# Folding the states into two chunks of the weights at once

## The chip, the cores and the metric

The kernel runs on one core of a Trainium2 chip. The metric is the time of one execution on the device in microseconds (us), taken as the median of several runs. A hardware profile of one further execution gives the spans, the rows and the order of events that are read below. TensorE is called PE there, its weight loads PEld, VectorE DVE, ScalarE ACT, GpSimd POOL, and the engine that issues most of the transfers SP.

## What is computed

Three layers follow each other, all in fp32. The second is where the change lies:

```python
scores = scale * np.matmul(x, state.transpose(0, 1, 3, 2))
a = softmax(scores)
xread = np.matmul(a, state)
sread = np.matmul(softmax(scale * np.matmul(state, x.transpose(0, 1, 3, 2))), x)
attn_out = np.concatenate([xread, sread], axis=2)

x = attn_out.transpose(0, 2, 1, 3).reshape(B * S, H * D)
x = (x @ w_a) * (x @ w_b) @ w_out

out[mask] = gate_w[mask, None] * (np.maximum(x[mask] @ w1[e], 0.0) @ w2[e])
```

There are 8 batches of 8 heads with 512 rows and 32 states of 64 numbers each. Each batch has 544 rows of 512 numbers (512 of xread, 32 of sread) for the second layer, whose inner width is 1536. The third layer sends each row to one of 8 experts by an argmax over its logits.

## The kernel before

Since xread is a @ state, the product xread @ w_a equals a @ (state @ w_a). The kernel never forms xread: it multiplies the states into the weights first ("folds" them) and applies the softmax to the result. The folded weights differ from batch to batch.

The second layer runs in blocks of 512 rows. Blocks i = 0 to 7 are the xread rows of one batch each, block 8 holds the 256 sread rows of all batches. The inner width is cut into 12 chunks, fc = 0 to 11, of 128 columns each of w_a and of w_b. A step is one chunk of one block, numbered 12 i + fc. `run` issues in each step what the string `STEP` lists:

```python
STEP = "mm1 fold a gc gm fh sg lt p mm2 lm b"
```

- `mm1` multiplies the block's softmax, split into a high and a low part AH and AL, by the folded weights of this chunk: 12 matmuls of 512 columns into the PSUM tiles pa and pb. Block 8 has plain weights, 256 rows and no fold.
- `fold` prepares the chunk two steps ahead. It multiplies the states by a chunk of the weights: 8 matmuls in fp32, for 4 pairs of heads j and 2 heads g, each on 64 rows and 32 columns of the array, with 256 columns moving (128 of w_a and 128 of w_b). They end in two PSUM tiles pm, one for each g.
- `gc` (copy_a) copies pa to SBUF on ScalarE; `gm` (times_b) multiplies it by pb on VectorE; `sg` splits the product into gh (ScalarE) and gl (VectorE).
- `fh` (folded) splits pm into high and low part: for each g a copy by ScalarE and a subtraction by VectorE, into a tile mm.
- `mm2` multiplies the product of the step before by w_out: 12 matmuls of 512 columns into po.
- `lt` and `lm` turn the finished rows of the block before for the logits (steps 1 to 4 of a block); `a`, `p` and `b` are places at which the attention of the next batch is issued (`PLAN`, `BATCH`): scores in step 0, directly behind the fold; the transposition of the second softmax (turn_s) in steps 3 and 7, its product with x (sread) in steps 4 and 8. `gate` runs after step 6 and `place`, which counts the ranks of the rows with matmuls of its own, after step 7.

Each engine works through its own queue in order. From step 14 to step 106 the order of the queues is that of the program; before and behind, a scheduler sets it. The tiles of pool `ps` (pa, pb, pm, and those of scores, turns and ranks, tag "ps") share four PSUM buffers of 2 KB in turn, so a new tile waits until the tile four places before it has been read. The pool `b2` gives mm two buffers.

The weights arrive as 64-bit numbers and are converted in the first block (`conv_pre`, `conv`) into one tile `ab0` to `ab11` of 4 KB for each chunk. In block 8 these are split on ScalarE and GpSimd (`split_w`), and the places of those no longer needed take the weights of the first expert, 16 tiles e0 to e15 of 4 KB, in the order of `SPACE` and not before the step that `READY` sets (`split_e0`). The third layer follows with queues of its own (`moe2`).

Of the kernel before, what the change touches and what calls it, by code (L numbers as in the profile page):

```python
# [7 lines left out]
F32 = mybir.dt.float32  # L8
F32R = mybir.dt.float32r
BF16 = mybir.dt.bfloat16  # L10
I32 = mybir.dt.int32
# [4 lines left out]
ALU = mybir.AluOpType  # L16
# [3 lines left out]
P = 128  # L20
# [8 lines left out]
CX = 320  # L29
# [20 lines left out]
)  # L50

SPACE = "ab0 ab1 wo0 ab2 ab3 wo1 ab4 wo2 ab5 ab6 wo3 ab7 ab8 ab9 ab10 ab11".split()
READY = 0, 0, 4, 6, 8, 9, 11, 12, 13, 14, 15, 16

BATCH = ("- - -", "- 0a 4p", "-2b -7a 0p")
# [2 lines left out]
def chunk(raw, c):  # L58
    g = raw[c // 2]
    return g[0][0][:, (c % 2) * 512 : (c % 2) * 512 + 512] if len(g) == 1 else g[c % 2][0]  # L60


class Front:


    def __init__(self, tc, ctx, xT, xN, sT, wab, wo, wgN, w1c, w2c, xs):
        self.__dict__.update(tc=tc, nc=tc.nc, xT=xT, xN=xN, sT=sT, wab=wab, wo=wo, wgN=wgN, w1c=w1c, w2c=w2c, xs=xs)
        nc = tc.nc
        self.V, self.A, self.G, self.PE = nc.vector, nc.scalar, nc.gpsimd, nc.tensor
        pool = lambda name, bufs, **kw: ctx.enter_context(tc.tile_pool(name=name, bufs=bufs, **kw))  # L70
        self.ctx = ctx
        self.cp = pool("c", 1)
        self.dp = pool("dram", 1, space=bass.MemoryType.DRAM)
        self.wp = pool("w", 1)
        self.p1 = pool("b1", 1)
        self.p2 = pool("b2", 2)
        self.at = pool("at", 2)
        self.ps = pool("psb", 4, space=PSUM)
        self.pso = pool("pso", 1, space=PSUM)
        self.sctx = ExitStack()  # L80
        self.sp = self.sctx.enter_context(tc.tile_pool(name="stg", bufs=2))
        self.us, self.xt, self.st, self.AB, self.WO, self.cvq, self.cvp = {}, {}, {}, {}, {}, [], []
        self.cvo = [0, 1] + [q for f in range(1, NF) for q in (3 * f, 3 * f + 1, 3 * f - 1)] + [3 * NF - 1]
        self.ahl, self.pm, self.MM = {}, {}, {}
        self.pab, self.g2, self.po, self.rows, self.lg, self.gt, self.ix, self.tp = {}, {}, {}, {}, {}, {}, {}, {}
        self.blocks = [(i * 512, 512) for i in range(8)] + [(4096, 256)]
        self.consts()
# [147 lines left out]
    def conv_pre(self):  # L235

        if not self.cvq:
            return
        q, raw = self.cvq.pop(0)
        fc, m = divmod(q, 3)  # L240
        r32 = raw.bitcast(I32).rearrange("p (n t) -> p n t", t=2)
        hi, lo = r32[:, :, 1], r32[:, :, 0]
        if m == 0:
            self.AB[fc] = self.wp.tile([P, 2, 512], I32, name=f"ab{fc}")
        w = self.AB[fc][:, m] if m < 2 else self.sp.tile([P, 512], I32, name="wt")
        self.A.activation(w.bitcast(F32), hi.bitcast(F32), AF.Copy, scale=2.0**-112)
        self.cvp.append((q, w, hi, lo))
# [15 lines left out]

    def fold(self, i, fc):

        pm = self.pm[i, fc] = [self.ps.tile([P, 256], F32, name=f"pm{g}", tag="ps") for g in range(2)]
        w, s = self.AB[fc].bitcast(F32), self.st[i]
        for j in range(4):
            for g in range(2):
                z = slice(64 * g, 64 * g + 64)  # L270
                self.PE.matmul(pm[g][32 * j : 32 * j + 32], s[z, j], w[z, :, j * P : j * P + P], start=True, stop=True)  # L271

    def folded(self, i, fc):
        m = self.MM[i, fc] = self.p2.tile([P, 2, 2, 256], F32R, name="mm")
        for g, t in enumerate(self.pm.pop((i, fc))):
            self.A.copy(m[:, 0, g], t)  # L276
            self.V.tensor_tensor(m[:, 1, g], t, m[:, 0, g], op=ALU.subtract)  # L277

    def load_xs(self):
        self.xsr = [self.at.tile([P, 2, 256], F32, name=f"xsr{a}", tag="eT") for a in range(2)]  # L280
# [82 lines left out]
    def turn_t(self, i, t, tag="ps"):  # L363

        tp = (self.ps if tag == "ps" else self.pso).tile([P, 512], F32, name="tp", tag=tag)
        for k in range(4):
            self.PE.transpose(tp[:, k * P : k * P + P], self.rows[i][:, t, k * P : k * P + P], self.ident)
        if t == 0:
            nt = self.blocks[i][1] // P
            self.x2 = self.lp.tile([P, 4, 512], F32, name="x2T") if nt == 4 else self.p2.tile([P, 2, 512], F32, name="x2T8", tag="mm")  # L370
        x = self.x2[:, t]
        if t % 2 == 0:
            self.A.copy(x, tp)
        else:
            self.V.tensor_copy(x, tp)
        self.tp[i] = tp
# [55 lines left out]

    def unit0_rows(self):
        p2 = self.p2
        r = p2.tile([P, 8, P], F32, name="rows0", tag="mm")
        self.load_rows(0, CW, r)
        xT = p2.tile([P, 1024], F32, name="xT0", tag="mm")
        th, tl = [p2.tile([P, 4, 8, 32], F32R, name=f"x0{n}", tag=n) for n in ("AH", "AL")]
        self.x0 = [[t[:, k] for k in range(4)] for t in (th, tl)]

        def turn0():
            self.turn_first(r, xT)
            self.turn_rows(1024, xT, *self.x0)

        self.turn0 = turn0
        self.mt = self.cp.tile([P, 3, 3, 2], F32, name="mt")
        r0 = self.first(0, E * REG - CW)
        self.m0 = self.cp.tile([P, 2, 2], F32, name="m0")
        self.nc.sync.dma_start(self.m0, self.xs[bass.ds(r0, CW), DM:RW].rearrange("(t p) c -> p t c", p=P))
# [96 lines left out]
    def split_e0(self):  # L546
        c = len(self.WH)
        if c >= 16:
            return
        t = self.wp.tile([P, 2, 512], F32R, name=f"e{c}", tag=SPACE[c])  # L550
        h, l = t[:, 0], t[:, 1]
        r = chunk(self.raw, c)
        self.A.copy(h, r)
        self.V.tensor_tensor(l, r, h, op=ALU.subtract)
        self.WH.append(h)
        self.WL.append(l)
# [140 lines left out]
    def run(self, order):  # L697
# [4 lines left out]
        def go(when):  # L702
            for f, a in sched.pop((st, when), []):
                f(*a)
# [22 lines left out]
        def logit():  # L727
# [4 lines left out]
            mm1=lambda: self.mm1(i, fc),  # L732
            mm2=second,
            fold=lambda: fold(self.fold),
            fh=lambda: fold(self.folded),
            gc=lambda: self.copy_a(i, fc),
            gm=lambda: self.times_b(i, fc),
# [6 lines left out]
            p=lambda: go("p"),  # L744
# [45 lines left out]
        i = nb - 1  # L790
# [10 lines left out]
        for t in range(2):  # L801
# [17 lines left out]
        self.unit0_mm2(0)  # L819
        self.unit0_mm2(1)  # L820
        x3 = self.lp.tile([P, 3, 2, CX], F32R, name="x3", tag="rows")
        x2 = [x3[:, k] for k in range(3)] + [self.p2.tile([P, 2, CX], F32R, name="x2", tag="mm")]
        xTh, xTl = [[x[:, q].rearrange("p (g t) -> p g t", t=32) for x in x2] for q in range(2)]
        self.turn_rows(4 * CX, wk[:, 2], xTh, xTl)
        self.mk = [self.PE.value_load(self.tab[0:1, 5 * NT + q : 5 * NT + q + 1], min_val=(0, 15)[q == 3], max_val=(2**NU - 1, NU)[q == 3]) for q in range(4)]
# [6 lines left out]
            xT=wk[:, 2],  # L832
            x2=x2,
# [437 lines left out]
```

## Time and profile before

| | |
|---|---|
| median of 3 runs | 1187.0 us (1183.28 to 1187.92) |
| profiled execution | 1186.3 us, span from first to last instruction 1184.5 us |
| TensorE busy | 1125.2 us, 95% of the span |
| VectorE busy | 751.1 us, 63% |
| ScalarE busy | 547.8 us, 46% |
| GpSimd busy | 242.6 us, 20% |
[...]

The times of runs include what lies around the span, 1.8 us in the profiled execution. The shares are means over stages that differ: conversion of the weights up to about 119 us, the blocks up to about 695 us, then block 8, the turn to the experts and the third layer.

### The profile page before, as it was taken

The numbers are of one execution on the slowest core, as the hardware profiler recorded it, in microseconds if no ns is written. First come the engines' busy times: TensorE is split into PE (matmuls) and PEld (weight loads), VectorE is DVE, ScalarE is ACT, GpSimd is POOL, SyncE is SP. The second block draws the span as 40 slices with busy tenths as digits, with TensorE's granted clock in tenths as the row PEclk, the third lists the DMA queues.
The fourth block names the chain that finished last, engine by engine and source line by source line (L and its number), as shares of the span: only waits on it lengthen the run. The fifth ranks groups of instructions, "written<-read, shape, count | busy, mean of one in ns | idle before, by whom it ended". The sixth has DMA issues, their size and how long they took to land. (4 is left out here: it accounts for less than half of the span.)

```text
span 1184.5 us, 21232 instructions
## 1 busy us (share of the span) xinstructions
PE 1125.2 (95%) x7867; PEld 899.3 (76%) x7867; DVE 751.1 (63%) x1585; ACT 547.8 (46%) x1171; POOL 242.6 (20%) x229
## 2 busy tenths in 40 slices
PE   3898999999999999999999998999999999999995
PEld 1565677777777777777777787889989898998995
DVE  6998554563664554555644436656887897777774
ACT  4554433432433333323333244425766767667663
POOL 1111001001000010010010143512434443434432
PEclk9998999999999999999999999999999999999998
DMA  7673822012011120120010041222765753154620
GB/s 288 191 247 120 183 53 75 1 37 76 1 50 63 38 63 15 38 75 1 2 55 1 19 143 37 59 62 62 205 192 165 220 160 101 43 170 95 186 59 26
DMA packets 68106, 108.79 MB, mean 92 GB/s; under 512 B 17266, under 2 KB 44146, under 8 KB 67970
## 3 DMA queue, kind: packets, MB, share of 16 engines
q1 hardware_dynamic: 61714, 89.11, 26.3%
q0 software_dynamic: 6256, 17.94, 4.0%
q8 instruction: 77, 1.26, 0.4%
q14 instruction: 59, 0.48, 0.1%
HBM read 83.30 MB, written 25.68 MB: 92 GB/s over the span
## 5 line engine op out<-in xcount | busy, mean ns | idle before, releaser
L322 DVE TENSOR_TENSOR g<-g,pb 128x512 f32<-128x512 f32 (+1 forms) x108 | 70.9, 656 | 222.1 <-PE pb L313 222.1
L337 PE MATMUL po<-wo,gh 128*128 128x512 f32 x408 | 170.9, 419 | 7.3 <-ACT gh L137 7.3
L318 ACT COPY g<-pa 128x512 f32<-128x512 f32 (+1 forms) x108 | 60.6, 561 | 227.8 <-PE pa L313 227.5
L338 PE MATMUL po<-wo,gh 128*128 128x512 f32 x408 | 161.4, 396 | 0.0
L339 PE MATMUL po<-wo,gl 128*128 128x512 f32 x408 | 159.8, 395 | 0.0
L524 POOL DMA_INDIRECT xs<-rows,ix x34 | 35.8, 1053 | 549.8 <-DVE AL L138 396.3
L978 PE MATMUL ph<-x,e 128*128 128x256 f32 (+1 forms) x480 | 138.6, 289 | 6.7 <-DVE e L1133 3.8
L980 PE MATMUL ph<-x,e 128*128 128x256 f32 (+1 forms) x480 | 138.7, 289 | 0.0
L979 PE MATMUL ph<-x,e 128*128 128x256 f32 (+1 forms) x480 | 138.5, 288 | 0.0
L276 ACT CAST mm<-pm 128x256 fp32r<-128x256 f32 x192 | 62.5, 375 | 122.3 <-PE pm L271 122.3
L337 PEld LDWEIGHTS po<-wo,gh 128*128 128x128 f32 x408 | 77.1, 189 | 44.9 <-issue 21.1
L978 PEld LDWEIGHTS ph<-x,e 128*128 128x128 f32 x480 | 91.7, 191 | 8.4 <-issue 7.9
L996 PE MATMUL pq<-e,h 128*128 128x512 f32 x240 | 93.4, 389 | 0.0
L995 PE MATMUL pq<-e,h 128*128 128x512 f32 x240 | 93.4, 389 | 0.0
L997 PE MATMUL pq<-e,h 128*128 128x512 f32 x240 | 93.4, 389 | 0.0
L979 PEld LDWEIGHTS ph<-x,e 128*128 128x128 f32 x480 | 91.6, 191 | 0.5
L980 PEld LDWEIGHTS ph<-x,e 128*128 128x128 f32 x480 | 91.8, 191 | 0.0
L339 PEld LDWEIGHTS po<-wo,gl 128*128 128x128 f32 x408 | 76.9, 189 | 18.7 <-DVE gl L138 0.8
L1166 DVE SCALAR_TENSOR_TENSOR h<-ph,h 128x256 fp32r<-128x256 f32 x120 | 50.5, 423 | 59.1 <-ACT h L1098 58.8
L338 PEld LDWEIGHTS po<-wo,gh 128*128 128x128 f32 x408 | 77.5, 190 | 13.1
L277 DVE TENSOR_TENSOR mm<-pm,mm 128x256 fp32r<-128x256 f32 x192 | 72.7, 418 | 22.2 <-ACT mm L276 22.2
L271 PE MATMUL pm<-ab,sT 64*32 64x256 f32 x1536 | 65.4, 398 | 18.8 <-DVE ab L258 17.0
(250 smaller groups left out, 2536.9 us busy)
## 6 DMA issues: line engine op xcount, KB each, us to landing
raw<-in_wab_dram SPq DMA_DIRECT2D x24, 512.0 KB, 4.4
wk<-xs SPq DMA_DIRECT2D x76, 160.0 KB, 3.7
xT<-in_xT_dram SPq DMA_DIRECT2D x16, 512.0 KB, 4.9
xn<-in_xN_dram SPq DMA_DIRECT2D x16, 512.0 KB, 4.6
er_x<-in_w1c_dram SPq DMA_DIRECT2D x16, 512.0 KB, 4.3
er_xn<-in_w1c_dram SPq DMA_DIRECT2D x16, 512.0 KB, 6.1
er_se<-in_w2c_dram SPq DMA_DIRECT2D x16, 512.0 KB, 4.5
er_y<-in_w2c_dram SPq DMA_DIRECT2D x16, 512.0 KB, 4.6
```

Of the source, the lines that this page charges most:

```text
L271: self.PE.matmul(pm[g][32 * j : 32 * j + 32], s[z, j], w[z, :, j * P : j * P + P], start=True, stop=True)
L277: self.V.tensor_tensor(m[:, 1, g], t, m[:, 0, g], op=ALU.subtract)
L322: self.V.tensor_tensor(g[:, :n], g[:, :n], pb[:, :n], op=ALU.mult)
L337: PE.matmul(o, gh[:, s], O[:, 0], start=fc == 0, stop=False)
L338: PE.matmul(o, gh[:, s], O[:, 1], start=False, stop=False)
L339: PE.matmul(o, gl[:, s], O[:, 0], start=False, stop=fc == NF - 1)
L978: e.matmul(o, WH[fc][:, c], xh, start=k == 0, stop=False)
L979: e.matmul(o, WL[fc][:, c], xh, start=False, stop=False)
L980: i = e.matmul(o, WH[fc][:, c], xl, start=False, stop=k == 3)
L995: e.matmul(o, hh[fc][:, z], WH[8 + fc], start=fc == 0, stop=False)
L996: e.matmul(o, hl[fc][:, z], WH[8 + fc], start=False, stop=False)
L997: i = e.matmul(o, hh[fc][:, z], WL[8 + fc], start=False, stop=fc == 7)
```

## The change

From block 1 on, `fold` works on two chunks at once in every even step, and does nothing in the odd ones. Its 8 matmuls have 512 moving columns, 256 of each chunk, and the two pm tiles fill a whole PSUM buffer. `folded` then splits both chunks in the same step, so the tag mm has three buffers. So that one access can reach two chunks, the converted weights lie in six tiles of two chunks (8 KB). The expert's tiles take them by halves, in another order (`SPACE`); e0 to e15 are due in the same steps. Block 0 folds chunk by chunk as before.

```diff
-SPACE = "ab0 ab1 wo0 ab2 ab3 wo1 ab4 wo2 ab5 ab6 wo3 ab7 ab8 ab9 ab10 ab11".split()
+SPACE = "ab0 ab0 ab1 ab1 wo0 wo1 ab2 ab2 wo2 wo3 ab3 ab3 ab4 ab4 ab5 ab5".split()
...
         if m == 0:
-            self.AB[fc] = self.wp.tile([P, 2, 512], I32, name=f"ab{fc}")
+            if fc % 2 == 0:
+                self.AB2[fc // 2] = self.wp.tile([P, 2, 2, 512], I32, name=f"ab{fc // 2}")
+            self.AB[fc] = self.AB2[fc // 2][:, fc % 2]
...
     def fold(self, i, fc):
 
-        pm = self.pm[i, fc] = [self.ps.tile([P, 256], F32, name=f"pm{g}", tag="ps") for g in range(2)]
-        w, s = self.AB[fc].bitcast(F32), self.st[i]
+        nf = 2 if i else 1
+        if fc % nf:
+            return
+        pm = [self.ps.tile([P, nf, 256], F32, name=f"pm{g}", tag="ps") for g in range(2)]
+        w, s = self.AB2[fc // 2].bitcast(F32)[:, fc % 2 : fc % 2 + nf], self.st[i]
         for j in range(4):
             for g in range(2):
                 z = slice(64 * g, 64 * g + 64)
-                self.PE.matmul(pm[g][32 * j : 32 * j + 32], s[z, j], w[z, :, j * P : j * P + P], start=True, stop=True)
+                o = pm[g][32 * j : 32 * j + 32].rearrange("p f (m c) -> p f m c", m=2)
+                self.PE.matmul(o, s[z, j], w[z, :, :, j * P : j * P + P], start=True, stop=True)
+        for f in range(nf):
+            self.pm[i, fc + f] = [t[:, f] for t in pm]
 
     def folded(self, i, fc):
-        m = self.MM[i, fc] = self.p2.tile([P, 2, 2, 256], F32R, name="mm")
-        for g, t in enumerate(self.pm.pop((i, fc))):
-            self.A.copy(m[:, 0, g], t)
-            self.V.tensor_tensor(m[:, 1, g], t, m[:, 0, g], op=ALU.subtract)
+        if i and fc % 2:
+            return
+        for f in range(fc, fc + (2 if i else 1)):
+            m = self.MM[i, f] = self.p2.tile([P, 2, 2, 256], F32R, name="mm", bufs=3)
+            for g, t in enumerate(self.pm.pop((i, f))):
+                self.A.copy(m[:, 0, g], t)
+                self.V.tensor_tensor(m[:, 1, g], t, m[:, 0, g], op=ALU.subtract)
...
-        t = self.wp.tile([P, 2, 512], F32R, name=f"e{c}", tag=SPACE[c])
+        k = SPACE[c]
+        if k[0] == "w":
+            t = self.wp.tile([P, 2, 512], F32R, name=f"e{c}", tag=k)
+        else:
+            if k not in self.e2:
+                self.e2[k] = self.wp.tile([P, 2, 2, 512], F32R, name=f"e{c}", tag=k)
+            t = self.e2[k][:, int(SPACE[c - 1] == k) if c else 0]
```

The lines of the changed program are numbered some 6 to 17 higher. The queue of TensorE in step 6 of block 5, from the last matmul of mm1 over the fold to the first of mm2, stands before as

```order
L313 MATMUL pb<-AL,mm 128x512
L271 MATMUL pm_4831<-ab_774,sT 32x256
L271 MATMUL pm_4832<-ab_774,sT 32x256
...
L337 MATMUL po_4523<-wo_665,gh 128x512
L338 MATMUL po_4523<-wo_665,gh 128x512
```

and now as

```order
L324 MATMUL pb<-AL,mm 128x512
L277 MATMUL pm_4545<-ab_770,sT 32x512
L277 MATMUL pm_4546<-ab_770,sT 32x512
...
L348 MATMUL po_4257<-wo_662,gh 128x512
L349 MATMUL po_4257<-wo_662,gh 128x512
```

The eight matmuls stay where they were and have 512 columns. In step 7 of the same block, the same queue, from mm1 over the turn of the softmax (pt) to mm2, stands before as

```order
L313 MATMUL pb<-AL,mm 128x512
L271 MATMUL pm_4904<-ab_855,sT 32x256
L271 MATMUL pm_4905<-ab_855,sT 32x256
...
L197 MATMUL pt<-ident,se 128x128 x4
L337 MATMUL po_4523<-wo_769,gh 128x512
```

and now as

```order
L323 MATMUL pb<-AH,mm 128x512
L324 MATMUL pb<-AL,mm 128x512
L197 MATMUL pt<-ident,se 128x128 x4
L348 MATMUL po_4257<-wo_765,gh 128x512
L349 MATMUL po_4257<-wo_765,gh 128x512
```

The fold of step 7 is gone. On VectorE the same two steps, from times_b (g) of step 6 over the softmax's normalization (sm, se) and the gate (down to rows) to the low part of g in step 7, stand before as

```order
L322 TENSOR_TENSOR g<-g,pb 128x512
L277 TENSOR_TENSOR mm<-pm_4831,mm 128x256
L277 TENSOR_TENSOR mm<-pm_4832,mm 128x256
L138 TENSOR_TENSOR gl<-g,gh 128x512
L182 TENSOR_SCALAR sm<-sm 128x1
...
L500 RECIPROCAL rows<-gm 128x4
L322 TENSOR_TENSOR g<-g,pb 128x512
L277 TENSOR_TENSOR mm<-pm_4904,mm 128x256
L277 TENSOR_TENSOR mm<-pm_4905,mm 128x256
L138 TENSOR_TENSOR gl<-g,gh 128x512
```

and now as

```order
L333 TENSOR_TENSOR g<-g,pb 128x512
L288 TENSOR_TENSOR mm<-pm_4545,mm 128x256
L288 TENSOR_TENSOR mm<-pm_4546,mm 128x256
L288 TENSOR_TENSOR mm<-pm_4545,mm 128x256
L288 TENSOR_TENSOR mm<-pm_4546,mm 128x256
L138 TENSOR_TENSOR gl<-g,gh 128x512
L182 TENSOR_SCALAR sm<-sm 128x1
...
L511 RECIPROCAL rows<-gm 128x4
L333 TENSOR_TENSOR g<-g,pb 128x512
L138 TENSOR_TENSOR gl<-g,gh 128x512
```

The two subtractions of step 7 stand in step 6 now, ahead of the low part of g and of all that follows it; ScalarE's copies moved in the same way. The queues of GpSimd and SP hold the same instructions in the same order.

## Rows read from the trace of the kernel before

**Rows 1.** Busy time by stage: us, then each engine's busy us (xinstructions), granted clock, DMA.

```profile
119.00:695.00 576.00, 576.00 (x4298) 420.78 (x4298) 301.24 (x728) 202.27 (x450) 35.71 (x44) 1.00 0.17 50
...
690.00:1184.50 494.50, 469.38 (x3009) 428.01 (x3007) 346.03 (x648) 287.83 (x610) 191.69 (x153) 0.98 0.40 114
```

**Rows 2.** Timeline, TensorE, a fold ahead of mm2: start us, us, instruction.

```profile
501.42 0.39 PE L312 MATMUL pb<-AH,mm 128*128 128x512 f32 x1
501.65 0.39 PE L313 MATMUL pb<-AL,mm 128*128 128x512 f32 x1
501.97 0.66 PE L271 MATMUL pm<-ab,sT 64*32 64x256 f32 x16
502.56 0.50 PE L337 MATMUL po<-wo,gh 128*128 128x512 f32 x1
502.90 0.39 PE L338 MATMUL po<-wo,gh 128*128 128x512 f32 x1
```

**Rows 3.** Timeline, TensorE, a fold ahead of turn_t.

```profile
554.85 0.39 PE L313 MATMUL pb<-AL,mm 128*128 128x512 f32 x1
555.17 0.66 PE L271 MATMUL pm<-ab,sT 64*32 64x256 f32 x16
555.77 0.66 PE L367 MATMUL tp<-ident,rows 128*128 128x128 f32 x4
556.18 0.48 PE L337 MATMUL po<-wo,gh 128*128 128x512 f32 x1
556.49 0.39 PE L338 MATMUL po<-wo,gh 128*128 128x512 f32 x1
```

**Rows 4.** Timeline, TensorE, turn_t in block 8, without a fold.

```profile
705.43 0.60 PE L367 MATMUL tp<-ident,rows 128*128 128x128 f32 x4
705.78 0.48 PE L337 MATMUL po<-wo,gh 128*128 128x512 f32 x1
706.10 0.39 PE L338 MATMUL po<-wo,gh 128*128 128x512 f32 x1
```

**Rows 5.** Timeline, TensorE, a fold ahead of the scores, then mm2.

```profile
540.83 0.66 PE L271 MATMUL pm<-ab,sT 64*32 64x256 f32 x16
541.29 1.55 PE L147 MATMUL ss<-xT,sT 64*32 64x512 f32 x16
542.77 0.51 PE L337 MATMUL po<-wo,gh 128*128 128x512 f32 x1
```

**Rows 6.** Instructions of the fold's and the scores' line: ns minimum/median/maximum, first and last start.

```profile
L271 PE MATMUL pm<-ab,sT x1536: 372/400/632, 14.7 to 682.7; 64*32 64x256 f32 x192
...
L147 PE MATMUL ss<-xT,sT x128: 589/613/1057, 6.0 to 542.2; 64*32 64x512 f32 x128
```

**Rows 7.** Timeline, TensorE, what is in flight at 541.6 to 541.7, and at 541.73 to 542.19.

```profile
541.29 0.59 PE L147 MATMUL ss<-xT,sT 64*32 64x512 f32 x1
...
541.29 1.12 PE L147 MATMUL ss<-xT,sT 64*32 64x512 f32 x9
```

**Rows 8.** Timeline, VectorE, times_b in the step with the scores; idle time in brackets.

```profile
541.01 0.69 DVE L322 TENSOR_TENSOR g<-g,pb 128x512 f32<-128x512 f32 x1 [3.82 <-PE pb L313]
```

**Rows 9.** Timeline, VectorE, steps 6 and 7 of block 5.

```profile
503.12 0.76 DVE L277 TENSOR_TENSOR mm<-pm,mm 128x256 fp32r<-128x256 f32 x2 [0.29 <-ACT mm L276]
...
508.45 0.56 DVE L497 TENSOR_TENSOR pre<-pre,oh 128x8 bf16<-128x8 bf16 x3
...
509.44 0.67 DVE L322 TENSOR_TENSOR g<-g,pb 128x512 f32<-128x512 f32 x1
```

**Rows 10.** Groups by line, 119 to 690 us: xcount | busy us, mean ns | idle us before.

```profile
L322 DVE TENSOR_TENSOR g<-g,pb 128x512 f32<-128x512 f32 x85 | 58.4, 687 | 208.0 <-PE pb L313 208.0
```

**Rows 11.** Timeline, TensorE, the rank matmuls after step 7 of block 5.

```profile
512.10 0.19 PE L509 MATMUL pk<-oh,tri 128*128 128x32 bf16 x1
```

**Rows 12.** Timeline, GpSimd (chunk 3 split) and ScalarE (e0 to e3), block 8.

```profile
707.64 2.54 POOL L138 TENSOR_TENSOR ws<-ab,ws 128x512 fp32r<-128x512 f32 x2 [1.85 <-ACT ws L137]
...
712.19 2.18 ACT L553 CAST e<-er_x 128x512 fp32r<-128x512 f32 x4
```

More of the change, by code (lines that the diff above doesn't have):

```diff
@@ L83, in __init__ @@
         self.cvo = [0, 1] + [q for f in range(1, NF) for q in (3 * f, 3 * f + 1, 3 * f - 1)] + [3 * NF - 1]
-        self.ahl, self.pm, self.MM = {}, {}, {}
+        self.ahl, self.pm, self.MM, self.AB2, self.e2 = {}, {}, {}, {}, {}
         self.pab, self.g2, self.po, self.rows, self.lg, self.gt, self.ix, self.tp = {}, {}, {}, {}, {}, {}, {}, {}
@@ L369, in turn_t @@
             nt = self.blocks[i][1] // P
-            self.x2 = self.lp.tile([P, 4, 512], F32, name="x2T") if nt == 4 else self.p2.tile([P, 2, 512], F32, name="x2T8", tag="mm")
+            self.x2 = self.lp.tile([P, 4, 512], F32, name="x2T") if nt == 4 else self.p2.tile([P, 2, 512], F32, name="x2T8", tag="mm", bufs=3)
         x = self.x2[:, t]
@@ L434, in unit0_rows @@
         p2 = self.p2
-        r = p2.tile([P, 8, P], F32, name="rows0", tag="mm")
+        r = p2.tile([P, 8, P], F32, name="rows0", tag="mm", bufs=3)
         self.load_rows(0, CW, r)
-        xT = p2.tile([P, 1024], F32, name="xT0", tag="mm")
+        xT = p2.tile([P, 1024], F32, name="xT0", tag="mm", bufs=3)
         th, tl = [p2.tile([P, 4, 8, 32], F32R, name=f"x0{n}", tag=n) for n in ("AH", "AL")]
@@ L821, in run @@
         x3 = self.lp.tile([P, 3, 2, CX], F32R, name="x3", tag="rows")
-        x2 = [x3[:, k] for k in range(3)] + [self.p2.tile([P, 2, CX], F32R, name="x2", tag="mm")]
+        x2 = [x3[:, k] for k in range(3)] + [self.p2.tile([P, 2, CX], F32R, name="x2", tag="mm", bufs=3)]
         xTh, xTl = [[x[:, q].rearrange("p (g t) -> p g t", t=32) for x in x2] for q in range(2)]
```

## The prediction

> **What bounds the kernel now.** I read four views, from coarse to fine. The stages come first: from 119 to 695 us TensorE is busy in all of 576 us at a granted clock of 1.00, while VectorE has work for 301 us and ScalarE for 202 [rows 1]. So nearly half of the kernel is a stretch in which TensorE never waits, and a microsecond taken off its queue there is a microsecond of the end, as long as nobody else starts to be waited for. Behind it, from 690 us on, TensorE is busy for 469 of 494.5 us [rows 1]; that part begins when the stretch ends.
>
> Then the timeline of TensorE around a fold, for what one fold costs the queue. The dense matmuls of 512 columns follow each other every 0.23 us. A fold that stands between mm1 and mm2 breaks that pace: from the start of the last mm1 matmul (501.65) to that of the second mm2 matmul (502.90) pass 1.25 us [rows 2], where two steps of the pace would take 0.46. **One fold costs 0.79 us.** Its 16 instructions (8 matmuls, two each for fp32) are shorter than that looks: where a group of the same 64x32 tiling follows, it starts 541.29 - 540.83 = 0.46 us after the fold does [rows 5], though one instruction alone lasts 0.40 [rows 6]. Eight run at once, in two rounds, and the rest of the 0.79 is leaving and entering the tiling.
>
> Where four transpositions follow the fold (turn_t, turn_s), the same distance is 556.49 - 554.85 = 1.64 us [rows 3]. In the last block, which has no fold, the first of them starts 706.10 - 705.43 = 0.67 us ahead of the second mm2 matmul [rows 4]; with one step of 0.23 from a 512-column matmul that is 0.90. A fold there costs 0.74 us.
>
> **The change, part by part.**
> *The odd steps lose their fold.* There are 42 such steps (11, 13, ... 93). In 22 the fold stands directly ahead of mm2, in 20 ahead of transpositions (14 of turn_t, 6 of turn_s). Taken off the queue: 22 x 0.79 + 20 x 0.74 = 32.2 us. It all lies on TensorE's queue in the stretch where TensorE is the bound.
>
> *The even steps get matmuls of 512 columns in place of 256.* No row of before shows a fold of 512 columns, but the scores have this very form: 64 rows, 32 columns of weights, 512 moving. One of their instructions has a median of 613 ns against 400 for the fold, and at the minimum 589 against 372 [rows 6]: 0.21 more either way. Two rounds make 0.43 us more for a fold. That it could be less no row suggests, since twice the columns have to pass. The other end is the whole group of scores: 542.77 - 541.29 = 1.48 us [rows 5], against 502.56 - 501.97 = 0.59 for a fold [rows 2], 0.89 more. I take 0.43: in the scores only one instruction is in flight at 541.6 us, and from 541.73 on the others come together [rows 7], and times_b, which frees the buffer of the second scores tile, runs from 541.01 for 0.69 us, to 541.70 [rows 8]. So the group's extra time is a wait for that buffer. The fold's two buffers were freed a step earlier. 36 even steps x 0.43 = 15.5 us.
>
> *In the other 6 even steps the scores follow the fold.* The larger fold takes 0.46 + 0.43 there and the scores start at 541.72 instead of 541.29, when times_b has just ended. Without the wait they need what a 512-column fold needs, 0.59 + 0.43 = 1.02, so mm2 starts at 542.74, against 542.77 now. I put these six at 0, with 0.43 each as the other end.
>
> **The sum:** 32.2 - 15.5 = 16.7 us less. The profiled execution took 1186.3 us (span 1184.5), which gives 1169.6; its time is 0.7 us below the median of 1187.0, so I say 1170.
>
> *The evacuation comes in fours.* Its instructions are the same in number and shape; what moves is when. In an even step the DVE queue holds four subtractions between times_b and the low part of g, and an odd step none. A pair of them takes 0.76 us [rows 9], so the last ends 0.43 (the larger fold) + 0.76 = 1.19 us later than now. Who waits for that? In most steps VectorE has stood idle before times_b, 208.0 us over 85 of them or 2.4 each [rows 10], and the buffers are wanted a step later: cost nothing, and the cover is that idle time. The tight place is step 6 of a block, where the softmax's normalization and the gate stand behind the subtractions. There times_b of step 7 starts at 509.44 [rows 9], without idle time before it, and the gate's last sum for the ranks (L497) is done at 508.45 + 0.56 = 509.01. TensorE wants it at 512.10 [rows 11]: 3.1 us of slack. After the change that sum is done 1.19 later, at 510.20, and TensorE arrives 0.74 - 0.43 = 0.31 earlier, at 511.79. 1.6 us are left, so I cost it at nothing.
>
> *The third buffer of mm* lets the copies of a pair be written while the second chunk of the last pair is still to be read; no new wait comes from it.
>
> *The weight tiles of two chunks* are reused in pairs by the first expert's tiles in the last block. The first pair whose turn is tight is e2 and e3 in the place of chunks 2 and 3: GpSimd splits chunk 3 from 707.64 for 2.54 us, to 710.18, and the copies of e0 to e3 start at 712.19 [rows 12]. 2 us of slack: cost nothing. SP and POOL issue what they issued.
>
> **The rivals.**
> *Part is given back at the gate.* If VectorE or ScalarE is later than I reckon in step 6, TensorE waits at the rank matmuls. For it: VectorE's queue has no idle time there. Against: the 1.6 us. If it costs the full shift of 1.19 + 0.31 = 1.5 us in each of 7 blocks, 10.5 us go back: 1180.
>
> *The larger folds cost what the scores cost.* If 0.89 is a property of 512 columns and not a wait, the even steps pay 42 x 0.89 = 37.4 us, more than the 32.2 saved: 1191.5, 0.4% above now. Against it stands that a single instruction is alone in flight until times_b ends [rows 7, 8].
>
> *The gain is lost behind the stretch.* If something after 690 us waited for a transfer and not for TensorE, the end would stay: 1186. Against: TensorE is busy for 95% of that part.
>
> *VectorE becomes the bound, the slower side.* Four subtractions in a row hold up times_b and the low part of g; if this makes mm1 or mm2 of the next step wait in every even step, 42 x 1.19 = 50 us are added: 1186.3 - 16.7 + 50 = 1220. It decides once the 2.4 us of idle time before times_b are used up; VectorE's 52% in the stretch speaks against that. [...]
>
> **How the numbers follow.** The forecast has 0.76, the gate 0.11, the costly folds 0.05, the loss behind the stretch 0.04, VectorE as the bound 0.04. The forecast's own range comes from 0.05 us of doubt on 84 prices, 4 us: 1165 to 1174. With the gate's case the range is 1165 to 1180, and 0.13 is left outside. A measurement can tell a change of about 0.5%, some 6 us, from none: forecast and gate are faster by more, 0.87; the costly folds and the loss behind it are within, 0.09; VectorE as the bound is slower, 0.04.
>
> **What would show it.** In the profile after: half as many fold instructions in the stretch, of 512 columns and about 0.61 us; a distance of about 1.68 us from the last mm1 matmul to the second mm2 matmul in an even step, 0.46 in an odd one; TensorE busy throughout a stretch some 16 us shorter; the scores' group shorter than 1.48 us; the rank matmuls about 1.6 us behind the gate's last sum. I am wrong if folds of 512 columns last as a group 1.4 us or more, if idle time of TensorE appears ahead of the rank matmuls, mm1 or mm2 with VectorE as its releaser, or if the part behind the stretch grows by what the stretch lost.

## The result and the profile after

The changed kernel takes 1174.57 us (median of 6 runs, 1172.52 to 1179.71) against 1187.29 in the runs of the kernel before beside it (1183.28 to 1189.23). The ratio is 0.991, interval 0.989 to 0.9929: 12.7 us less, where the prediction had 1170 and 16.7. The profiled execution took 1174.63 us, its span 1172.8.

The timeline of TensorE in steps 5 to 7 of block 5 answers to [rows 2]. First comes step 5, without a fold (last matmul of mm1, first two of mm2), then step 6 with the pair, then the turn of the softmax and the first rank matmul of step 7:

```profile
486.00 0.39 PE L324 MATMUL pb<-AL,mm 128*128 128x512 f32 x1
486.23 0.40 PE L348 MATMUL po<-wo,gh 128*128 128x512 f32 x1
486.46 0.40 PE L349 MATMUL po<-wo,gh 128*128 128x512 f32 x1
...
491.53 0.39 PE L324 MATMUL pb<-AL,mm 128*128 128x512 f32 x1
491.85 1.09 PE L277 MATMUL pm<-ab,sT 64*32 64x512 f32 x16
492.87 0.50 PE L348 MATMUL po<-wo,gh 128*128 128x512 f32 x1
493.21 0.39 PE L349 MATMUL po<-wo,gh 128*128 128x512 f32 x1
...
498.48 0.60 PE L197 MATMUL pt<-ident,se 128*128 128x128 f32 x4
...
501.69 0.19 PE L520 MATMUL pk<-oh,tri 128*128 128x32 bf16 x1
```

From mm1's last matmul to mm2's second pass 0.46 us in the odd step and 493.21 - 491.53 = 1.68 in the even one, the two numbers that the prediction named. Where the scores follow the fold (the same view, to be held against [rows 5]), the lone scores instruction is gone, the group lasts 531.70 - 530.64 = 1.06 us, and from the fold to mm2 pass 1.94 us as before:

```profile
529.76 1.09 PE L277 MATMUL pm<-ab,sT 64*32 64x512 f32 x16
530.64 1.12 PE L147 MATMUL ss<-xT,sT 64*32 64x512 f32 x16
531.70 0.51 PE L348 MATMUL po<-wo,gh 128*128 128x512 f32 x1
```

The line of the fold (beside [rows 6]) has 864 instructions instead of 1536, with a median of 589 ns; the forms are a sample:

```profile
L277 PE MATMUL pm<-ab,sT x864: 373/589/632, 14.8 to 662.2; 64*32 64x512 f32 x134, 64*32 64x256 f32 x39
```

VectorE has 164.3 us of idle time before 85 times_b, 1.9 each, instead of the 2.4 of [rows 10] (groups by line, 119 to 675 us):

```profile
L333 DVE TENSOR_TENSOR g<-g,pb 128x512 f32<-128x512 f32 x85 | 58.4, 687 | 164.3 <-PE pb L324 161.2 <-ACT g L329 1.7 <-issue 0.3
```

The turn_t of block 8 without a fold, at 705.43 in [rows 4], comes at 690.70, 14.7 us earlier:

```profile
690.70 0.60 PE L378 MATMUL tp<-ident,rows 128*128 128x128 f32 x4
```

So up to there all went as predicted. Put matmul beside matmul in the two traces, and the lead is 16.2 us at 860 us of the kernel before, 14.2 at 900, and 11.3 from 960 to the last unit. That it first grows from 14.7 to 16.2 is not the change's doing: the kernel before has one stretch more at the lower level of TensorE's clock (0.50 of full speed for 3.4 us, from 723.73 on), behind 3.73 us of which TensorE was busy for 1.47. The column behind POOL is the granted clock:

```profile
723.80:727.00 3.20, 3.04 (x37) 2.69 (x38) 1.06 (x4) 1.03 (x2) 2.06 (x2) 0.50 0.02 5
```

Not every execution has as much of it: for another of the kernel before (e_before_p127, below) the mean granted clock is 0.989, against 0.986 here. Some 5 us are then given back at two places of the third layer. Both show in the waits of TensorE's weight loads behind 785 us (801 in the kernel before): two waits for nothing that the profile shows, 8.2 us together, where the kernel before had two of 4.6 together. First after, then before:

```profile
PEld ph L995 <- issue: 8.2, 2, 5.2
```

```profile
PEld ph L978 <- issue: 4.6, 2, 3.0
```

TensorE's sequencer is in the branch to the next expert's unit. The rows of the branch at the end of a unit, first after, then before (ns, minimum/median/maximum), show that most take 0.37 us and one 4.99 (2.87 before); the second long one takes 2.98 (1.71 before):

```profile
L1070 PEldq COMPARE_BRANCH  x16: 77/370/4987, 794.7 to 1128.8; - x16
```

```profile
L1053 PEldq COMPARE_BRANCH  x16: 77/372/2871, 810.9 to 1140.1; - x16
```

The page's group of that matmul names another culprit:

```profile
L995 PE MATMUL ph<-x,e 128*128 128x256 f32 (+1 forms) x480 | 139.3, 290 | 10.5 <-DVE e L1150 7.4
```

The matmul's last semaphore came from VectorE's cast of the expert's weights, so the wait is put down to it. The row of the weight load says "issue", and the long branch ahead of it fits that: by this reading the instruction had not reached the engine. After both long branches of the change the granted clock is 0.50 for 3.4 us (864.85 to 868.26 and 933.12 to 936.53); ahead of the first TensorE had stood idle for 4.77 us. Two stretches of 4 us of the change (in the kernel before the first wait was followed by 0.59 from 880 to 884 us, the second by 1.00 from 944 to 948):

```profile
864.00:868.00 4.00, 2.54 (x12) 2.57 (x13) 4.00 (x6) 1.36 (x3) 1.68 (x1) 0.61 0.48 82
...
932.00:936.00 4.00, 4.00 (x25) 4.00 (x24) 4.00 (x7) 2.36 (x5) 3.24 (x3) 0.64 0.81 118
```

### The profile page after: what moved, and what is told of

Same layout as the page of the kernel before. It is cut to its first block, busy times and chain, and to the rows that moved or that the text cites. A ratio compares the mean times of both kernels' runs of the same rounds, so it can differ in the third digit from the quotient of the medians.

```text
span 1172.8 us, 19968 instructions
## 1 busy us (share of the span) xinstructions
PE 1111.0 (95%) x7195; PEld 895.8 (76%) x7195; DVE 750.5 (64%) x1585; ACT 551.5 (47%) x1171; POOL 243.0 (21%) x229
## 5 line engine op out<-in xcount | busy, mean ns | idle before, releaser
L348 PE MATMUL po<-wo,gh 128*128 128x512 f32 x408 | 168.1, 412 | 6.6 <-ACT gh L137 6.6
L349 PE MATMUL po<-wo,gh 128*128 128x512 f32 x408 | 160.5, 393 | 0.0
L137 ACT CAST gh<-g 128x512 fp32r<-128x512 f32 (+1 forms) x108 | 64.5, 597 | 101.1 <-DVE g L333 101.0
L348 PEld LDWEIGHTS po<-wo,gh 128*128 128x128 f32 x408 | 77.0, 189 | 42.3 <-issue 18.9
L138 DVE TENSOR_TENSOR gl<-g,gh 128x512 fp32r<-128x512 f32 (+1 forms) x108 | 71.7, 664 | 42.1 <-ACT gh L137 38.3
```

What stands on the lines that cost most here:

```text
L138: eng.tensor_tensor(l, raw, h, op=ALU.subtract)
L348: PE.matmul(o, gh[:, s], O[:, 0], start=fc == 0, stop=False)
L349: PE.matmul(o, gh[:, s], O[:, 1], start=False, stop=False)
```

## The experiments

Each ratio is to runs of the kernel before on the same chip (medians of 1186.9 to 1188.0 us). The theory on the stretch: what a fold costs is entering and leaving the 64x32 tiling, and it is now paid once for two chunks. On the loss, theories were formed one after the other.

**e_layout**: the tiles of two chunks, the order of the expert's tiles and the third mm buffer, but one chunk folded in each step.

```diff
-        nf = 2 if i else 1
+        nf = 1
...
-        if i and fc % 2:
-            return
-        for f in range(fc, fc + (2 if i else 1)):
+        for f in range(fc, fc + 1):
```

> The layout alone: tiles of two chunks, three buffers of mm and the new places of the expert's tiles, but one fold of 256 columns in every step, as before. If the gain comes from the folds alone (my theory), this takes what before takes, within 0.3%, and its folds cost the queue 0.79 us each. If the layout itself gained or lost time (rival), it stands 4 us or more off. For the loss of 5 us in the third layer: if it hangs on the shorter program of TensorE, this program, as long as before's, waits for the branch behind the small units as before did (2.9 and 1.7 us); if it hangs on the new places of the expert's tiles, it waits like the change (5.0 and 3.0).

1186.69 us against 1187.86, ratio 0.9989 (0.9974 to 1.0004). Its two long branches took 2.77 and 1.97 us, near those of the kernel before. The layout is worth nothing and does not lengthen the branches; the gain hangs on folding in pairs.

**e_two_groups**: a pair is folded in one step, but with 256-column matmuls, twice as many.

```diff
-        for j in range(4):
-            for g in range(2):
-                z = slice(64 * g, 64 * g + 64)
-                o = pm[g][32 * j : 32 * j + 32].rearrange("p f (m c) -> p f m c", m=2)
-                self.PE.matmul(o, s[z, j], w[z, :, :, j * P : j * P + P], start=True, stop=True)
+        for f in range(nf):
+            for j in range(4):
+                for g in range(2):
+                    z = slice(64 * g, 64 * g + 64)
+                    o = pm[g][32 * j : 32 * j + 32, f].rearrange("p (m c) -> p m c", m=2)
+                    self.PE.matmul(o, s[z, j], w[z, f, :, j * P : j * P + P], start=True, stop=True)
```

> The changed kernel, but the two chunks of an even step are folded by 16 matmuls of 256 columns in a row instead of 8 of 512. If the gain is that the 64x32 tiling is entered and left once per pair (my theory), little is lost: four rounds of 0.23 us against two of 0.45, so a fold of 0.46 + 0.59 = 1.05 us against 1.02, 42 x 0.03 = 1.3 us more than the change in the stretch. If the wider matmul itself is the gain (rival), the stretch gives back most of it, 10 us or more. The program of TensorE is as long as before's: if the waits for the branch in the third layer hang on that, they are 2.9 and 1.7 us again, and this kernel is as fast as the change or faster by some 2 us.

1173.03 us, ratio 0.9873 (0.9851 to 0.9895). The timeline of TensorE around such a fold:

```profile
493.64 0.39 PE L325 MATMUL pb<-AL,mm 128*128 128x512 f32 x1
493.95 1.09 PE L278 MATMUL pm<-ab,sT 64*32 64x256 f32 x32
494.98 0.50 PE L349 MATMUL po<-wo,gh 128*128 128x512 f32 x1
495.32 0.40 PE L350 MATMUL po<-wo,gh 128*128 128x512 f32 x1
```

The distance is 1.68 us again, with 32 instructions instead of 16. So the wide matmul is worth nothing in the fold itself; what is saved is the second place in the stream. A fold of one chunk costs 0.79 us [rows 2] and a second chunk in the same group 1.68 - 1.25 = 0.43 more, so that some 0.36 us of each group, by this estimate, are entering and leaving the other tiling; no run takes such a change of the tiling by itself. The lead at turn_t of block 8 is smaller than the change's all the same (11.9 us against 14.7). Of the 2.9 us, 0.6 lie ahead of the first pair, and some 1.5 in step 8 of the blocks, where the product of the second softmax with x, directly behind the fold, goes on for 0.83 us instead of 0.58; why, no run shows. Here that group and the first of mm2 behind it, in e_two_groups and then in the change:

```profile
507.85 0.91 PE L220 MATMUL pr<-xn,eT 128*32 128x64 f32 x32
508.68 0.50 PE L349 MATMUL po<-wo,gh 128*128 128x512 f32 x1
...
505.70 0.65 PE L220 MATMUL pr<-xn,eT 128*32 128x64 f32 x32
506.28 0.50 PE L348 MATMUL po<-wo,gh 128*128 128x512 f32 x1
```

Yet the kernel is no slower. From turn_t on it takes 479.9 us where the change takes 482.1, and its branches took only 1.66, 1.28 and 1.68 us. This made the branches the suspects.

**e_after_again**: the changed kernel once more, unaltered.

> The changed kernel once more, for a second trace of it. If the longer waits for the branch behind the small units belong to the program, they are within 0.3 us of 5.0 and 3.0 again and TensorE falls to half its clock behind both; if they are chance, they differ by a microsecond or more, and so does the distance between the end of the stretch and the end of the kernel.

1175.97 us (1174.17 to 1181.01), ratio 0.9892 (0.9875 to 0.9909); in its profile, of the slowest of its five runs (1181.01 us), the branches took 5.04 and 4.00 us, and the clock fell behind both (0.91 on average from 840 to 880 us and from 920 to 960, against 0.96 for both in the change). The first is within 0.3 us of 4.99, the second is 1.0 off 2.98, the mark that the expectation set for chance. So long branches at these two places belong to the program; how long the second is varies.

**e_after_no_loads**: the transfers that the waits might be for are taken away.

```diff
-                    with e.If(fl > 0):
+                    with e.If(fl > 1):
```

> The changed kernel without the transfers of the later experts' weights in the third layer (all units compute with the first expert's). If TensorE waits behind the small units because the code of the next unit comes late beside these transfers (my theory), the two branches take 0.4 us like the others, TensorE keeps its clock there, and the kernel is 7 to 11 us faster. If the wait is for something else (data of the weights split by VectorE, say), it stays about as long.

1171.77 us, ratio 0.9871 (0.9854 to 0.9889). The branch:

```profile
L1070 PEldq COMPARE_BRANCH  x16: 77/374/3747, 794.9 to 1125.0; - x16
```

Without transfers the first branch still takes 3.75 us (the second 0.76), and the kernel is 4.2 us faster than e_after_again beside it, not 7 to 11. The expectation of 0.4 was missed: the transfers lengthen the waits, but the first is there without them.

The trace has instruction transfers too, in a queue of their own (q8) with packets of 16 KB. Their number goes with TensorE's instructions, so they are read as its code: from 130 to 690 us, where few branches stand, there are 33 of them for 8349 matmuls and weight loads in the kernel before, 29 for 7211 in the change and 34 for 8485 in e_two_groups, one for some 250 each time (253, 249 and 250). The 256 that the expectations below reckon with is the author's estimate near these counts; no run shows it exactly. So the next theory was that TensorE waits for code, and that the code's place in the program decides. **e_pad64, e_pad128, e_pad192, e_pad256** move TensorE's code of the third layer by 63, 127, 191 and 255 instructions, with a block that is never entered:

```diff
+                fork(masks[3], "IS_GT", 1000, "never", "unit0")
+                place("never")
+                e.wait_ge(s_xl, 0)
+                for q in range(31):
+                    e.matmul(ph[0][:, :CW], WH[0][:, 0:P], x2[0][:, 0, :CW], start=True, stop=True)
+                e.br("pe_unit0")
                 for u in range(NU - 1):
```

(31 matmuls; 63, 95 and 127 in the others.)

> The change, with a branch ahead of the third layer on TensorE to a block that is never entered: 31 matmuls that move TensorE's code of the third layer back by 63 instructions, about as far as the version with 256-column folds in pairs has it (64). No work and no transfer changes. Theory (the two long waits at TensorE's branches into the next unit, 4.99 and 2.98 us, depend on where the code lies in the program): waits near those of that version, 1.7 and 1.3 us, and a time of about 1170, 4 to 5 us under the change. Rival (the waits belong to what the transfers or VectorE do at that moment): the waits stay 5.0 and 3.0 us and the time stays about 1175.

> As the run before with 63 never-entered matmuls, TensorE's code of the third layer 127 instructions further back than in the change. Theory (place of the code): other lengths than 5.0 and 3.0 us at the two branches, or a wait at another unit; the sum of the long waits may lie anywhere from 1 to 10 us, and the time goes with it, 1168 to 1178. Rival: 5.0 and 3.0 us at the same two units, about 1175.

> As the run before with 95 never-entered matmuls, 191 instructions further back than in the change. Theory (place of the code): the waits differ again from 5.0 and 3.0 us, and the time follows their sum, 1168 to 1178. Rival: 5.0 and 3.0 us, about 1175.

> As the run before with 127 never-entered matmuls, 255 instructions further back than in the change, which is 16 KB of code, one packet of the instruction transfers in the trace. Theory (place of the code, by its position within such a packet): the code lies within a packet where it lay in the change, so the waits come back to about 5.0 and 3.0 us and the time to about 1175, although it is the largest shift. Rival (the shift as such, or an extra branch, changes the waits): they keep the direction that 63, 127 and 191 showed.

| version | us, median | ratio to before (interval) |
|---|---|---|
| e_pad64 | 1172.24 | 0.9881 (0.9865 to 0.9897) |
| e_pad128 | 1177.86 | 0.9933 (0.991 to 0.9956) |
| e_pad192 | 1171.26 | 0.987 (0.9856 to 0.9884) |
| e_pad256 | 1177.02 | 0.9931 (0.9918 to 0.9944) |

The branches of e_pad64, e_pad192 and e_pad256, in this order:

```profile
L1070 PEldq COMPARE_BRANCH  x16: 77/382/1582, 795.7 to 1127.1; - x16
```

```profile
L1070 PEldq COMPARE_BRANCH  x16: 77/368/1309, 796.5 to 1126.4; - x16
```

```profile
L1070 PEldq COMPARE_BRANCH  x16: 77/365/4391, 798.2 to 1130.2; - x16
```

In the first two the longest branch is another, further on (at 950 and at 1104 us); the two that were long take 1.00 and 1.10 us, and 0.36 each. A shift by 63 or 191 shortens the long branches, a shift by 255, about a whole packet by these counts, brings them back (4.39 and 2.97), and the time of these three follows: with no work changed, e_pad192 and e_pad256, on the same chip, lie 5.8 us apart with intervals that don't touch. The extra branch is in all of them and is not the cause. e_pad64 has 3.7 us of "issue" ahead of its weight loads instead, 1.9 the longest. In e_pad128 the two branches take 0.36 and 0.38 us (a later one, at 1065 us, takes 3.16, but TensorE is busy for 39.90 of the 40 us from 1040 to 1080), and its weight loads wait for 6.1 us in all with "issue", the longest of them in the midst of a unit (the number in brackets is the idle time):

```profile
854.82 0.19 PEld L992 LDWEIGHTS ph<-x,e 128*128 128x128 f32 x1 [2.05 <-issue]
```

That stop ends 2.35 us after a packet has started. So a shift can move the waits into the units, and the two branches alone do not set the time: e_pad128 is as slow as e_pad256. It is also the widest of all, 1172.04 to 1182.99 in 7 runs. e_pad192 beats both kernels. It has waits at the same places still, but others (TensorE's weight loads behind 785 us):

```profile
PEld ph L995 <- DVE h L1188: 3.1, 2, 2.5
PEld ph L995 <- DVE x L1168: 2.1, 2, 1.0
```

Where the long branches are gone, VectorE's part of the hidden layer is the releaser of the longest wait, 2.5 us. 5.2 us of waits stay, as against 8.2 in the change and 4.6 in the kernel before, and the gain of 1186.86 - 1171.26 = 15.6 us is about what the stretch gives.

Last, whether place within a packet is the whole rule. **e_before_p169, e_before_p233, e_before_p127** are the kernel before with the same block (84, 116 and 63 matmuls), **e_pad23** the change with 11.

> The kernel before (one chunk per fold, no change), with 84 never-entered matmuls and a branch ahead of TensorE's third layer: its code there lies 169 instructions further back, so that it stands within the 256 instructions of a 16 KB packet (23 further than the change, and 169: 192) where the version of the change moved by 191 has it, the fastest so far. Theory (place of the code, independent of the folds): the two long waits at the branches, 2.87 and 1.71 us in the kernel before, shrink to one of about 1.3 us or none, and the time falls by 2 to 4 us to 1183 to 1185; the change at the same place (1171.3) would then be 12 to 14 us faster, and not 16, or 16 if the half-clock stretch behind the waits goes too (1187). Rival (the folds made the waits, by starting the third layer 16 us earlier): waits as in the kernel before, about 1187.

> The kernel before with 116 never-entered matmuls, 233 instructions further back: within a packet its third layer then stands where the change has it (23 and 233: 256). Theory (place of the code): waits of about 5.0 and 3.0 us at the same two branches and a time of 1189 to 1193, 2 to 5 us slower than the kernel before. Rival: waits of 2.9 and 1.7 us, about 1187.

> The change with 11 never-entered matmuls, 23 instructions further back: within a packet its third layer then stands where the kernel before has it. Theory (place of the code): the waits of the kernel before, 2.9 and 1.7 us, and a time of 1170 to 1173, 15 to 17 us under the kernel before, which is what the prediction's sum had. Rival: 5.0 and 3.0 us, about 1175 to 1177.

> The kernel before with 63 never-entered matmuls and a branch, TensorE's third layer 127 instructions further back. The kernel before kept its two waits at shifts of 0, 169 and 233 (2.87 and 1.71; 3.87 and 2.21; 3.25 and 2.03 us); the change has them at 0, 23 and 255 and not at 63, 127 and 191. Theory (a band of places within the 256 instructions of a packet brings the waits; 0, 169 and 233 of the kernel before all lie in it, which needs a band of at least 87 instructions, and the change allows up to 128): 127 lies outside it, the two waits fall below 1.2 us each or move into a unit or to another branch, and the time falls by 1 to 4 us, 1184 to 1187. Rival (in the kernel before the waits have another cause and no place removes them): 2.9 to 3.9 and 1.7 to 2.2 us, 1187 to 1188.

In all four the rival was right. They gave, in this order, 1187.76 (ratio 1.0001, 0.9989 to 1.0012), 1186.76 (0.9991, 0.998 to 1.0002), 1175.95 for e_pad23 (0.9911, 0.9886 to 0.9936) and 1188.46 (1.001, 0.9997 to 1.0023). The branch of e_before_p127, which should have been free:

```profile
L1053 PEldq COMPARE_BRANCH  x16: 77/377/4411, 808.2 to 1138.9; - x16
```

So the rule fell. In the kernel before, four places gave two long branches each time, and the time did not move; in the change 0, 23 and 255 have them and 63, 127 and 191 do not. That the two programs share one rule by place was wrong. What all runs share is in the table: the two branches' times, and when a 16 KB packet of instructions started, counted from the branch's start (us; both are read from the records of the trace).

| version | first branch | packet | second branch | packet |
|---|---|---|---|---|
| before | 2.87 | +0.5 | 1.71 | -0.6 |
| e_layout | 2.77 | +0.2 | 1.97 | -0.4 |
| e_before_p127 | 4.41 | +1.7 | 1.69 | -0.7 |
| e_before_p169 | 3.87 | +1.4 | 2.21 | -0.1 |
| e_before_p233 | 3.25 | +0.8 | 2.03 | -0.3 |
| the change | 4.99 | +2.4 | 2.98 | +0.6 |
| e_after_again | 5.04 | +2.6 | 4.00 | +1.4 |
| e_pad23 | 4.50 | +1.9 | 3.48 | +1.1 |
| e_pad256 | 4.39 | +1.8 | 2.97 | +0.6 |
| e_after_no_loads | 3.75 | +1.1 | 0.76 | -1.6 |
| e_pad64 | 1.00 | -1.4 | 1.10 | -1.3 |
| e_two_groups | 1.66 | -1.3 | 1.28 | -1.1 |
| e_pad128 | 0.36 | -3.6 | 0.38 | -3.8 |
| e_pad192 | 0.36 | -8.2 | 0.36 | -6.8 |

Wherever a branch in the table takes over 0.4 us, it ends 2.3 to 3.0 us after the packet's start, and so do all others of over 1 us behind these. The last unit of every kernel has one of 3.4 to 3.9 us, whose packet starts 0.9 to 1.5 us after the branch. In e_pad192 both packets had come long before. What makes a packet start at +2.4 here and at -8.2 there is left open: in the change some places of the code bring it early, in the kernel before none of the four did, and leaving out the weight transfers brings it from +2.4 to +1.1.

## Why the prediction was right, and what was missing

**The folds: right.** The even step costs 1.68 us, the odd one 0.46, and the steps with scores 0.02 to 0.05 more than before, each about as worked out. The two rounds are in the traces: eight of a fold's instructions start within 0.05 us, and the other eight 0.24 us behind them with 256 columns and 0.45 with 512. The first group of a pair starts at 120 us. Ahead of it the changed kernel is 0.9 us behind (mm1 at 117.33 against 116.45), where traces of the change differ by more (115.44 in e_pad23, 117.77 in e_pad192); at turn_t of block 8 it is 14.7 ahead. The stretch gained 15.6 us (15.0 to 15.6 in the seven other profiles that fold in this way); the sum had 16.7. From step to step, the odd ones gave 32.1 us, against 32.2 in the sum, and the even ones cost 16.5 instead of 15.5: 0.46 in most, not 0.43. 1.1 us over 84 steps is 0.013 each, inside the 0.05 allowed.

**The costly folds: fell.** With times_b out of the way, scores of 512 columns take 1.06 us as a group, and not 1.48; 0.43 was the right end.

**The evacuation in fours: right at nothing.** The timeline of VectorE in step 6 shows the four subtractions in a row and the gate's sum:

```profile
492.03 0.69 DVE L333 TENSOR_TENSOR g<-g,pb 128x512 f32<-128x512 f32 x1 [3.40 <-PE pb L324]
493.44 1.62 DVE L288 TENSOR_TENSOR mm<-pm,mm 128x256 fp32r<-128x256 f32 x4 [0.72 <-ACT mm L287]
...
499.67 0.56 DVE L508 TENSOR_TENSOR pre<-pre,oh 128x8 bf16<-128x8 bf16 x3
```

The sum is done at 500.23, and TensorE wants it at 501.69: 1.5 us of slack where 1.6 were forecast. The rival at the gate fell with that, and so did VectorE as the bound: TensorE is busy for 575.79 of 576 us from 119 to 695.

```profile
119.00:695.00 576.00, 575.79 (x3729) 430.24 (x3728) 305.97 (x736) 213.60 (x466) 42.72 (x52) 1.00 0.17 51
```

**Behind the stretch: the term that was mis-sized.** The prediction costed that part at nothing: "TensorE is busy for 469 of 494.5 us [rows 1]; that part begins when the stretch ends". From turn_t of block 8 to the end it takes 482.1 us, where it took 479.0. It has two branches that, by this reading, wait for code, and they went from 2.87 + 1.71 to 4.99 + 2.98 us, 3.4 more. The lower clock behind the second branch, 3.4 us of it, costs 1.7 us by estimate, about what the kernel before lost by its own further stretch of lower clock. So the spans differ by 15.6 - 0.9 - 3.1 = 11.6 us. The step that failed is the reading of 25 us of idle time as something that moves along unchanged: it was not asked what ended the longest of it. The rival "lost behind the stretch" had the place, and a transfer as the wait, but did not think of code: without the weight transfers the first branch still took 3.75 us. Where the packets come ahead of the branches (8.2 and 6.8 us in e_pad192) the gain is 15.6 us, 1.1 short of the sum.

**The range: in part luck.** 1174.57 us lie 0.6 above the forecast's own range (1165 to 1174) and inside the wide one only because that was drawn for the gate's case, which did not occur. Nothing in the prediction held the loss behind the stretch to 3 us: by the place of the code alone the changed kernel takes 1171.3 to 1177.9 us.

That the place of the code sets the long branches of the change is shown by its shifts, which alter nothing else. That what they wait for is a late packet of code is read from the fixed distance between the two in all 14 profiles; why some of these shifts bring the packet early and none in the kernel before is not shown.

## What to carry to other kernels

Count the entries into a foreign tiling, and not only its matmuls: where a small tiled group stands in a dense stream, two groups in one place cost 1.22 us where two places cost 1.58. An edit that only changes how many instructions an engine has also moves the code behind it; here such a shift alone moved the time by up to 6 us (1171.3 to 1177.9), far from the edit, so compare such versions with a never-entered block of two or three sizes before a few us are put down to the edit. And where the page names an engine as the releaser of a wait, look at the weight load and the sequencer's branch ahead of it: a wait of microseconds with "issue" behind a long branch was, by the packets' times, one for code here. A short one need not be: TensorE's weight loads in the change have some of up to 0.8 us between 119 and 690 us, too.

## What was not expected

That TensorE would wait for its own code, as the times suggest: branches of 0.37 us took up to 5.04 us, and the long ones always ended 2.3 to 3.0 us after a 16 KB packet of instructions had started. The page of the change counts 72 of them (77 in the kernel before):

```profile
q8 instruction: 72, 1.18, 0.4%
```

That these packets are what the long branches wait for is a reading of three measurements: one packet for some 250 of TensorE's instructions, up to 5.04 us where a branch takes 0.37, and the distance of 2.3 to 3.0 us from the packet's start to the branch's end. No run takes the packets away. Stops of up to 2.05 us came inside units as well. Why the kernel before kept its waits at four places of its code stays open.
